# A new order table for the same operations: gated linear recurrence followed by a gMLP block

## The chip, the cores and the metric

The kernel runs on one core of a Trainium2 chip. The metric is the device time of one execution in microseconds (us). The kernel before took 147.5 us, the median of three runs (146.93, 147.5 and 147.93). Its profile comes from a further execution, whose span, from the first instruction to the last, is 146.7 us. Times inside the profile are counted from the start of that span.

## The reference, cut to what matters

```python
def _attn_ref(q, k, v, alpha):           # all (4, 8, 768, 48)
    for t in range(S):
        state = alpha[:, :, t, :, None] * state + np.einsum('bhd,bhe->bhde', k[:, :, t], v[:, :, t])
        y[:, :, t] = np.einsum('bhd,bhde->bhe', q[:, :, t], state)

def _moe_ref(x, w_in, w_spatial, b_spatial, w_out):   # x is y as (4, 768, 384)
    h = np.maximum(x @ w_in, 0.0)        # (4, 768, 1024): u and v, 512 each
    v_n = (v - mu) / np.sqrt(var + 1e-06)
    v_s = np.einsum('ts,bsd->btd', w_spatial, v_n) + b_spatial[None, :, None]
    return ((u * v_s) @ w_out).astype(np.float32)
```

A recurrence over 768 steps with a decay for each of 48 rows of the state, for 4 batches and 8 heads, is followed by a block that mixes over time (w_spatial is 768 x 768) and projects back to 384.

## The kernel before, in words

**Tiling.** The recurrence is cut into 24 chunks of 128 time steps, six for each batch. Chunks 0 to 5 are worked in pairs, with loads of 384 KB for two chunks; chunks 6 to 23 are worked singly, each with four loads of 192 KB: `ac` (alpha), `kc` (k), `qc` (q) and `vc` (v). A single load brings rows of 48 numbers, 192 bytes each. Six weight loads of 768 KB and 24 stores of 192 KB make up the rest of the transfers. All but a 1.5 KB one are issued by SyncE into one queue, in one order.

**Operations.** The body makes no schedule. It builds a list of 1108 operations, each with a key, the engines that may do it, and what it depends on. For chunk i the ones that matter here are:

- `ln.i` (ScalarE, from `ac`), then `cum.i` (TensorE, the decay sums), then three exponentials on ScalarE;
- `kt.i` (GpSimd, from `kc`) and `qt.i` (VectorE, from `qc`), then `trk.i` (TensorE, eight transposes, those of k first), `ev.i` (copy out), `sc.i` (scores, TensorE), `m.i` (mask, VectorE);
- `vb.i` (GpSimd or ScalarE, from `vc`), then `upd.i` (TensorE, from `kt` and `vb`), `z.i` (VectorE), `S.i` and `sb.i` (GpSimd): the state of chunk i as weights for chunk i+1;
- `y.i` (TensorE, from `m.i`, `vb.i` and `sb.(i-1)`), then `xs.i`, `xt.i`, `xe.i`: the output turned into the layout that the second part reads.

For batch b the second part has `v.b.t` (6 products with half of w_in, each with statistics `bn`, `rs`, `vn`), `u.b.f.h` (8 products with the other half), `s.b.f.h` (8 products with w_spatial, each in two parts of three matmuls), `g.b.f.h` (the gate, GpSimd or VectorE) and `o.b.t` (6 products with w_out), followed by the store `st.b.t`. An output tile waits in a buffer until it is stored; the pool `outp` has four of them, and tile (3,0) takes the buffer of tile (2,2).

**Order.** `replay` walks through the string `PLAN`. A word is a letter for the engine and the number of the operation: `G758` emits operation 758, which is `kt.17`, on GpSimd. `S749` is the issue of the load `kc.17`, and the word `Q750` stands where the planner had the transfer itself begin. Numbers after a colon are columns of matmuls on a constant tile, with no use for the result, that are put on TensorE ahead of the operation (`fill`, line 188). Every engine runs its words in the order of the string; what an engine waits for, all behind it waits for. The table was computed ahead of time by a planner that isn't in the file. It used the durations that the operations carry, among them

```python
    LD, LP, WT, ST = 1.03, 1.46, 2.35, 0.8
```

for the transfer of a single-chunk load, of a pair load, of a weight load and of a store. These numbers are data for the planner; the emitted program doesn't use them.

Lines that the profile names: 188 constant-tile matmuls, 361 `xt`, 417 and 616 `ln`, 464 and 646 `kt`, 471 and 656 `qt`, 602 single load, 672 and 674 `trk`, 690 `upd`, 704 `sc`, 732 and 726 `y`, 778 all products of the second part, 332 `S`, 198 copies on VectorE and GpSimd (`vb`, `sb`, `ev`), 933 `g`, 980 store.

Of the kernel before, what the change touches and what calls it, by code (L numbers as in the profile page):

```python
# [54 lines left out]
LETTERS = {"P": "PE", "D": "DVE", "A": "ACT", "G": "POOL", "S": "SP", "Q": "DMA"}  # L55

PLAN = """
S34 S96 G0 S36 S38 Q35 D1 Q97 S100 A42 Q37 S98 P43:512:512:512:512:512:512:512:512:512:352 A104 G32 P54:512 Q33 A44
Q39 S40 P116 A55 D47 A56 P105:128 A57 G58 A45 A46 D2 Q101 S166 P50:512:96 A107 A106 P61:256 A117 D51 A118 A108 D59
A119 Q99 S102 D48 P63:512:512:512:512 A64 D121 P243:512:224 P52 D110 P125 Q41 S4 D53 D62 A126 P73:512:512:160 G120  # L60
P114 A244 D74 P76 Q167 G109 S168 P123:160 D115 D75 A49 G60 P112:512:512:192 D77 Q103 A113 P65:224 S170 D78 A124
P135:512 D66 A174 P79:96 D136 G67 Q5 S172 P138 A80 D137 G68 P69:224 A111 D70 G122 D139 P83:512:352 G71 D140 P175 G72
Q169 S9 P127 A177 A84 P81 D128 P141 A82 G129 A176 P85 Q171 S303 P186 A142 D7 G6 A86 P131 D8 A178 P143 D130 G179 A187
P87 Q173 S14 A188 D132 P90 A88 G133 D180 P145 A91 G189 D190 Q10 S305 A144 P182 D92 P184 A146 G134 P194 A185 P149
D195 G181 A183 D89 P147 P192 G191 A148 P200 G3 Q304 A193 S307 P245:128 D201 P160 A150 D202 Q15 P203 P196 D12 A13 D11
A246 D205 P156:512:512:512:512:320 S18 A93 P154 D197 A311 Q306 S309 D204 A161 G198 P152 A157 P312 D16 Q308 G199 S335
A155 P206 D151 A313 G17 Q19 A153 P210 D94 A314 A207 G315 D162 S22 P158 A316 P208 A211 P233 D317 A209 P231 D95 A163
P212 Q310 P319 D232 S337 A213 P214 D164 A234 G20 D320 Q336 P223 S370 A215 G21 D159 P217 Q23 D216 S339 P227 A218 P235
A224 P237 D219 A228 P225 A318 P229 D165 A343 Q338 D236 S341 P325 A220 D238 P321 A226 P344 Q371 D222 P259 A230 S372
D221 P251 A346 A345 D326 Q340 A24 G25 P255 S374 D322 P256 D327 A348 Q342 P260 G347 S412 D257 P239 A378 Q373 P328  # L70
G323 P241 S410 A240 D349 P379 P252 Q375 D261 A380 S414 P247 A381 D242 A329 G262 Q413 P248 A350 D253 S376 A383 P351
D249 G324 Q411 P353 P330 D352 S26 P267 A331 G258 P268 D384 Q415 S445 P357 G382 D269 P275 Q377 A418 D354 S416 P276
D359 G355 P386 Q27 D358 G356 S447 P271 D387 P419 G254 P272 A421 D277 A420 P392 A423 G422 P332 D424 P360 D273 G250
Q446 A333 S449 P426 D393 A361 P263 G274 A385 Q417 D394 P264 S477 A427 P388 P362 D265 Q448 P395 S479 A363 D31 P432
G266 D30 A396 P364 Q450 D29 A28 S481 D389 A453 D334 P397 P279 G390 Q478 A398 S572 G391 A365 P454 D433 P399 Q480 A455
D434 G278 S451 A456 A458 P408 A400 Q482 P283 D459 G425 S574 A280 D401 G457 P404 A284 Q573 P287 S604 A485 D409 G270
A405 Q452 P428 D366 P486 A288 S576 P435 A487 P461 Q575 A436 G488 S483 P291 A367 D462 A489 Q605 P295 D369 S578 A292
D429 P437 D490 A296 Q577 P467 G430 S606 A438 P406 D368 G431 A580 D469 P492 Q484 A407 S608 P581 D468 G460 P439 A582
Q579 D493 A583 S641 A585 P463 G584 P470 D464 A612 Q607 P494 D586 A471 S639 P402 G465 D495 A440 P472 Q609 G466 P613
A403 D496 S679 P588 A615 A614 G491 P299 D441 Q642 A473 S610 G587 A617 P497 G616 D589 Q640 P474 A498 S681 D618 A442  # L80
P590 P499 Q680 D591 P594 A500 S715 P620 G592 D596 A300 Q611 P501 A475 D443 S645 A476 D621 P514 Q682 P508 S643 D595
A502 P512 A503 Q716 G619 D444 S683 D515 P626 A647 P597 D504 P524 Q646 A513 S717 P528 A598 A509 Q644 D627 P540 S685
A505 P648 A687 P599 D507 Q684 P510 A600 D506 S719 P688 A649 D628 P525 Q718 A650 A690 A652 G651 S747 P541 D526 A723
P622 Q686 P529 D542 A689 G593 S749 A692 P544 D623 D530 Q720 A654 G691 P545 S751 D693 P629 D653 Q748 G624 P724 S841
P695 D511 A725 G543 P655 A630 Q750 D546 P516 S873 A726 A728 G527 P631 D696 A656 Q752 P517 S721 G625 P657 D729 P601
A632 Q842 D658 A694 G531 S843 D518 P661 A602 P701 Q874 D662 P633 G727 A755 S845 D663 P520 Q722 A634 G519 D702 S875
P756 P521 A757 Q844 D703 G659 P664 S877 P536 D522 G758 A665 Q846 P731 D635 A759 S753 P532 G660 A849 Q876 D760 P666
P697 S912 G547 P533 A667 D698 A732 Q878 P537 D534 S908 G523 P704 D538 P850 Q754 A705 P668 D603 G699 S948 A851 P762
A852 Q913 A854 G853 S847 P677 A669 D855 P706 Q909 A730 P548 G700 D678 S301 A707 D763 P733 Q949 P857 A549 D734 S879
A881 P708 D858 G735 A670 Q848 P737 S983 G535 P764 A709 D739 P863 Q302 P671 A710 S914 G736 D738 Q880 P552 S910 A636  # L90
D765 G761 P740 A672 Q984 G539 D766 P882 S950 A741 P556 A553 D864 Q915 G856 P767 S1015 A557 D865 P742 P560 A884 A768
Q911 D711 A883 S952 P673 A886 G885 P564 Q951 A743 D887 S985 A916 P769 D637 G888 P859 A561 Q1016 P675 D674 G923 S954
A770 P744 D676 A712 Q953 P777 D860 S987 A745 D638 P889 G861 Q986 A565 P771 S1019 A956 D890 A778 P779 Q955 D746 A772
S289 P917 P891 P957 A919 Q988 A918 D713 P866 S989 D714 A959 P781 A780 G920 D773 A921 Q1020 P793 S1021 A867 P797 D892
A1023 Q290 D922 P568 A774 S293 Q990 A958 P924 S1017 D776 A961 P785 D775 G960 Q1022 A782 D925 P868 S285 P786 A869
D962 G893 P794 Q294 A963 D787 G862 P798 A569 Q1018 D795 A991 P870 S570 G788 D799 S297 Q286 P926 A871 P895 D927 G796
P930 Q571 D897 P801 Q298 G894 P802 D896 P783 D932 G928 P992 D931 P789 A994 A993 P898 D803 A784 G995 P1024 A996 P966
P933 A899 D967 P790 D997 A934 G968 P809 A1025 D791 G998 A1027 P900 P810 D872 G1026 A901 P964 D1028 P999 G800 A965
P813 D1000 G792 P935 P1030 D811 A936 P814 D1031 G804 P1001 P817 D1002 G929 D815 P970 A818 P1005 D971 P1032 G1003
P942 G1029 D972 P821 G816 D1006 P805 A822 D1007 G969 P973 P937 D1033 A974 G1004 P806 D1034 A938 P975 P1008 D807 A976  # L100
P902 D943 A1009 G808 D939 P1035 A903 P1010 P977 G812 A1036 D904 P944 A978 P940 A1011 D979 P1037 P829 A1038 D945 A905
P825 D907 P1012 A826 A980 P1039 A941 D981 P1049 A1013 D982 P946 D906 A1040 D1014 P1045 A830 P1051 A947 S831 D1041
A1046 P1047 S281 P1053 S823 D1050 A1042 Q832 S558 P1057 A1052 D1044 Q282 S827 P1077 A1048 D1043 Q824 S562 P1065 Q559
P1078 S819 P1066 Q828 P1061 Q563 D1067 P1054 Q820 G1068 P1058 D1055 P1062 D1059 G1056 P1069 D1060 P1070 D1063 P1073
D1079 P833 P1074 A834 P1081 D1075 S835 P1082 D1064 S550 G1076 P837 S554 D1071 Q836 S566 P1084 D1080 A838 Q551 G1072
P1088 S839 Q555 D1083 A1085 P1092 Q567 S1086 A1089 Q840 P1100 S1090 A1093 Q1087 P1096 S1094 A1101 Q1091 P1104 S1102
A1097 Q1095 S1098 A1105 Q1103 S1106 Q1099 Q1107
"""


# [973 lines left out]
```

## Time and profile before

| what | value | where |
|---|---|---|
| time | 147.5 us (146.93 to 147.93) | three runs |
| TensorE busy | 138.6 us of 146.7 | page, first part |
| first and last TensorE matmul | 1.32 us, ends at 143.02 us | chain of waits |
| transfers | 28.61 MB, 93,014 packets, 87,872 of them under 512 B | transfers |
| median single load, issue to landing | 3.8 to 4.2 us | issues |
| median store from `o_sb`, issue to landing | 2.4 us | issues |
| granted TensorE clock | 0.997 | run's record |

In the page, the first part gives busy time by engine and the second the same in 40 slices of 3.67 us, as tenths; `DMA` is the mean busy share of the 16 transfer engines. A matmul's busy time includes its way through the array, so that neighbours overlap: a full slice says that work was under way, and the pace is read from the distance of starts. In the list of stretches, `x` is the number of instructions, `DMA share` the busy share of the transfer engines. In the list of instructions by time, a bracket gives the idle time of the engine before the instruction and what ended it.

### The profile page before, as it was taken

To read this page: it belongs to the slowest core of one execution; us is meant where nothing else is said; L and a number is where in the kernel's file an instruction comes from. 1 tells how busy PE (TensorE), PEld (TensorE's weight loads), DVE (VectorE), ACT (ScalarE), POOL (GpSimd) and SP (SyncE) were. 2 spreads that over 40 slices of the span, in tenths; PEclk is the share of its full clock that TensorE was granted. 3 is DMA by queue.
4 is the path that set the end of the run, shared out by engine and by line. 5 is a ranking of instruction groups with operands and counts; after the bars stand their busy time and mean duration, and the time that the engine had idled before them with its cause. 6 is when DMAs were issued, how large, how long until landed. Compare 5 with 4: busy or idle time off the path is not lost.

```text
span 146.7 us, 4486 instructions
## 1 busy us (share of the span) xinstructions
PE 138.6 (94%) x1702; PEld 92.3 (63%) x1715; DVE 120.6 (82%) x260; ACT 107.8 (73%) x271; POOL 87.1 (59%) x148
## 2 busy tenths in 40 slices
PE   6999999999999999995998999999999999999990
PEld 3567776676666666773666577666667766566550
DVE  6578989979999899994977898988989999767820
ACT  3595779988984599995996889999948548860160
POOL 5726487574258959773139987853597994004320
PEclk9999999999999999999999999999999999999998
DMA  4999998978997999997998999999998000063384
GB/s 109 268 261 263 330 259 245 332 183 210 312 216 151 267 208 199 197 197 141 191 213 163 221 194 206 186 210 188 202 222 258 22 0 0 4 242 138 135 293 161
DMA packets 93014, 28.61 MB, mean 195 GB/s; under 512 B 87872, under 2 KB 91456, under 8 KB 92992
## 3 DMA queue, kind: packets, MB, share of 16 engines
q1 hardware_dynamic: 92960, 28.32, 83.4%
q8 instruction: 13, 0.21, 0.6%
q14 instruction: 9, 0.07, 0.2%
q0 software_dynamic: 32, 0.00, 0.0%
HBM read 23.60 MB, written 4.72 MB: 193 GB/s over the span
## 4 chain that ended last, share of the span: by engine, by line
PE 64%; DMA 12%; DVE 8%; ACT 5%; POOL 4%; issue 3%; SPq 1%; DVEq 0%; ACTq 0%; POOLq 0%
PE bank L778 38%; DMA qc<-in_q_dram 7%; PE bank L188 6%; DMA raw_w<-in_moe_w_spatial_dram 5%; PE bank L704 2%; POOL gT L933 2%; PE bank L672 2%; PE bank L732 2%; PE bank L361 2%; PE bank L674 2%; PE bank L690 1%; DVE qt L656 1%; PE bank L492 1%; PE bank L428 1%; SPq L602 1%
## 5 line engine op out<-in xcount | busy, mean ns | idle before, releaser
L778 PE MATMUL bank<-w_spT,vn 128*128 128x384 bf16 x192 | 36.3, 326 | 0.0
L933 POOL TENSOR_TENSOR gT<-vsb,uT 128x384 bf16<-128x384 f32 x28 | 25.8, 932 | 16.1 <-DVE vsb L920 15.5
L778 PEld LDWEIGHTS <-vn 128*128 128x128 bf16 x192 | 17.3, 97 | 10.0 <-issue 0.2
L715 DVE TENSOR_TENSOR ptm<-bank,mask 128x512 bf16<-128x512 f32 x36 | 22.8, 681 | 0.5 <-PE bank L704 0.5
L646 POOL TENSOR_TENSOR kt<-kc,binv 128x384 bf16<-128x384 f32 x18 | 16.7, 928 | 7.4 <-ACT bc L641 4.4
L920 DVE TENSOR_TENSOR vsb<-bank,bsp_bc 128x384 f32<-128x384 f32 x31 | 16.7, 552 | 3.8 <-PE bank L778 2.8
L778 PE MATMUL bank<-xT,w_in 128*128 128x384 bf16 x96 | 19.2, 327 | 0.0
L778 PE MATMUL bank<-w_out_sb,gT 128*128 128x384 bf16 x96 | 18.4, 326 | 0.1
L778 PE MATMUL bank<-w_in,xT 128*128 128x512 bf16 x59 | 17.1, 379 | 1.0 <-issue 0.5
L332 POOL TENSOR_TENSOR state<-state,bc 128x192 f32<-128x192 f32 x20 | 10.2, 511 | 8.2 <-DVE state L327 4.9
L198 POOL CAST sbd<-state 64x192 bf16<-64x192 f32 x38 | 12.9, 340 | 2.0
L196 ACT COPY xT<-bank 128x384 bf16<-128x384 bf16 x24 | 11.7, 487 | 3.0 <-PE bank L361 2.4
L839 DVE BATCH_NORM_STATS2 stats<-v_sb 128x6 f32<-128x512 bf16 x20 | 13.6, 682 | 0.3 <-ACT v_sb L202 0.3
L202 ACT ACTIVATE v_sb<-bank 128x512 bf16<-128x512 f32 x20 | 11.7, 598 | 2.6 <-PE bank L778 2.2
L656 DVE TENSOR_TENSOR qt<-qc,bank 128x384 bf16<-128x384 f32 x18 | 9.8, 548 | 4.4 <-DMA qc<-in_q_dram 2.9
L188 PE MATMUL bank<-junk 128*128 128x384 bf16 (+5 forms) x66 | 11.8, 313 | 1.3 <-DVE junk L231 1.3
L198 DVE COPY kqT<-bank 128x1024 bf16<-128x1024 bf16 (+1 forms) x19 | 11.6, 614 | 1.5 <-PE bank L674 0.5
L196 ACT COPY o_sb<-bank 128x384 f32<-128x384 f32 x9 | 4.3, 480 | 11.4 <-PE bank L778 11.4
L778 PEld LDWEIGHTS <-w_in 128*128 128x128 bf16 x96 | 8.7, 98 | 6.1
L778 PEld LDWEIGHTS <-gT 128*128 128x128 bf16 x96 | 9.0, 97 | 5.4 <-issue 0.3
L196 ACT CAST x_sb<-bank 128x384 bf16<-128x384 f32 x24 | 11.6, 488 | 1.0 <-PE bank L732 0.5
L871 DVE TENSOR_SCALAR vn<-v_sb,mvs,rstd 128x512 bf16<-128x512 bf16 x24 | 10.6, 467 | 2.0 <-ACT rstd L864 1.9
(124 smaller groups left out, 299.1 us busy)
## 6 DMA issues: line engine op xcount, KB each, us to landing
ac<-in_alpha_dram SPq DMA_DIRECT2D x18, 192.0 KB, 4.1
kc<-in_k_dram SPq DMA_DIRECT2D x18, 192.0 KB, 3.9
qc<-in_q_dram SPq DMA_DIRECT2D x18, 192.0 KB, 3.8
vc<-in_v_dram SPq DMA_DIRECT2D x18, 192.0 KB, 4.2
raw_w<-in_moe_w_spatial_dram SPq DMA_DIRECT2D x3, 768.0 KB, 7.6
out_dram<-raw_w SPq DMA_DIRECT2D x12, 192.0 KB, 2.3
out_dram<-o_sb SPq DMA_DIRECT2D x9, 192.0 KB, 2.4
raw_w<-in_moe_w_in_dram SPq DMA_DIRECT2D x2, 768.0 KB, 7.6
```

The source lines that it names most:

```text
L188: nc.tensor.matmul(out=flat[:, 0:n], lhsT=junk[:, 0:128], rhs=junk[:, 0:n], start=True, stop=True)
L196: nc.scalar.copy(out=out, in_=in_)
L198: ENG[eng].tensor_copy(out=out, in_=in_)
L202: nc.scalar.activation(out=out, in_=in_, func=AF.Relu)
L646: ENG[eng].tensor_mul(out=k_blocks(kt3)[:, :, :, 0:D], in0=quad(st["kc"]), in1=st["binv"])
L656: nc.vector.tensor_mul(out=qt[:, :, ::-1, 0:D], in0=quad(st["qc"]), in1=st["cv"])
L715: nc.vector.tensor_tensor(out=st["ptm"][:, s], in0=st[f"pt{s}"], in1=mask4, op=ALU.mult)
L778: return lambda ps: nc.tensor.matmul(out=out(ps), lhsT=lhsT(), rhs=rhs(), start=start, stop=stop)
L839: nc.vector.bn_stats(out=stats, in_=d["v_sb"][:, tt, :])
L871: nc.vector.tensor_scalar(out=d["vn"][:, t, :], in0=d["v_sb"][:, t, :], scalar1=d["mvs"][:, t, 0:1], scalar2=d["rstd"][:, t:t + 1], op0=AL ...
L920: nc.vector.tensor_tensor(out=hold["vs"], in0=ps[:, 0:TH], in1=bsp_bc[:, th, :], op=ALU.add)
L933: ENG[eng].tensor_tensor(out=bt[b]["gT"][:, dsl, cols], in0=hold["vs"], in1=bt[b]["uT"][:, dsl, cols], op=ALU.mult)
```

## The change

The string `PLAN` is replaced by another one for the same 1108 operations; nothing else in the file changes. The new table comes from a planner run with longer times for single-chunk loads and for stores; the constants in the file are as they were. It is meant to fit the order to transfers that take longer than the old table took for granted. The diff replaces 50 lines by 50 others; its beginning:

```diff
-S34 S96 G0 S36 S38 Q35 D1 Q97 S100 A42 Q37 S98 P43:512:512:512:512:512:512:512:512:512:352 A104 G32 P54:512 Q33 A44
-Q39 S40 P116 A55 D47 A56 P105:128 A57 G58 A45 A46 D2 Q101 S166 P50:512:96 A107 A106 P61:256 A117 D51 A118 A108 D59
...
+S34 S96 G0 S36 S40 Q35 D1 Q97 S38 A42 D2 Q37 S100 P54:512:512:512:512:512:512:512:512:512:352 A104 G32 P43:512 Q33
+Q41 S98 P116:512 A44 A55 P105:128 G47 A118 Q39 S166 A106 G58 A49 P50:512:512:192 A57 A51 Q101 G60 S102 A45 A46
...
```

With numbers turned into names, the order of SyncE where the two tables differ most, from the 45th transfer on:

```
before: qc.12 vc.11 vc.12 kc.13 qc.13 kc.14 ac.14 ac.15 vc.13 kc.15 ac.16 vc.14 qc.14 qc.15 kc.16 vc.15 qc.16 ac.17 kc.17 qc.17 ac.18
after:  qc.12 vc.11 ac.14 qc.13 kc.13 vc.12 qc.14 kc.14 ac.15 ac.16 vc.13 ac.17 kc.15 qc.15 vc.14 ac.18 vc.15 kc.16 qc.16 qc.17 kc.17
```

The words of TensorE and GpSimd around chunk 15 (`s.1.3.1/1` is the second part of that product):

```
TensorE before: s.1.0.1 xt.14 upd.15 s.1.0.1/1 s.1.1.1/1 y.15 cum.18 v.2.2 trk.17 u.2.3.0 xt.15 o.1.0
TensorE after:  xt.14 trk.16 sc.15 u.2.0.0 v.2.2 u.2.1.0 upd.15 trk.17 y.15 cum.18 u.2.3.0 o.1.0 xt.15
GpSimd before:  sb.13 g.1.3.0 kt.16 g.1.0.0 S.14 kt.17 sb.14 g.1.3.1 g.1.1.0 S.15 kt.18 sb.15 S.16 g.1.0.1 sb.16
GpSimd after:   vb.15 kt.16 g.1.2.0 kt.17 S.14 sb.14 g.1.0.0 vb.16 g.1.2.1 kt.18 S.15 vb.17 sb.15 g.1.3.1 S.16 sb.16
```

And the end of TensorE's list:

```
before: s.3.3.1 s.3.3.1/1 o.2.5 o.3.0 o.3.1 o.3.2 o.3.4 o.3.3 o.3.5
after:  s.3.2.1/1 s.3.1.1/1 o.3.0 o.3.1 s.3.3.1/1 o.3.2 o.3.3 o.3.4 o.3.5
```

A few operations change engine where the list allows two: one `sb` on VectorE becomes four, eleven `ev` on ScalarE become fourteen, three gates on VectorE become two, eight weight casts on VectorE become seven. The constant-tile matmuls go from 16,224 to 16,704 columns.

## The prediction

> **What bounds the kernel now.** I read the page first, its busy times and its slices.
>
> ```profile
> PE 138.6 (94%) x1702; PEld 92.3 (63%) x1715; DVE 120.6 (82%) x260; ACT 107.8 (73%) x271; POOL 87.1 (59%) x148
> ...
> PE   6999999999999999995998999999999999999990
> ...
> DMA  4999998978997999997998999999998000063384
> ```
>
> Two things are full: TensorE nearly everywhere, and the transfer engines until about 112 us, when the last load lands. TensorE has one hole, slice 19, near 67 us. The stretches of ten microseconds (columns: TensorE, weight loads, VectorE, ScalarE, GpSimd, clock, transfer share, GB/s) show it as 8.32 of 10, while transfers go on:
>
> ```profile
> 60.00:70.00 10.00, 8.32 (x124) 5.91 (x125) 7.79 (x18) 8.31 (x24) 6.00 (x13) 1.00 0.92 177
> 70.00:80.00 10.00, 9.63 (x108) 6.16 (x106) 8.04 (x20) 8.50 (x26) 4.88 (x9) 1.00 0.96 189
> 80.00:90.00 10.00, 9.89 (x125) 6.83 (x127) 9.08 (x19) 8.64 (x20) 8.99 (x14) 1.00 1.03 201
> ```
>
> The instructions by time name the waits inside:
>
> ```profile
> 68.36 0.36 PE L690 MATMUL bank<-vb,kt 128*128 128x48 bf16 x8 [1.09 <-POOL vb L198]
> ...
> 69.67 0.38 PE L672 MATMUL bank<-ident,kt 128*128 128x128 bf16 x4 [0.46 <-DVE qt L656]
> ...
> 79.47 0.40 PE L674 MATMUL bank<-ident,qt 128*128 128x128 bf16 x4 [0.30 <-DVE qt L656]
> ```
>
> The chain of waits (start, duration) runs through two loads there, and after them through TensorE alone:
>
> ```profile
> 63.81 5.16 DMA qc<-in_q_dram
> ...
> 73.89 4.87 DMA qc<-in_q_dram
> 78.86 1.03 DVE qt L656 x2
> ...
> 125.97 17.06 PE bank L778 x101
> ```
>
> So the end is TensorE's own work plus the time for which loads held it up.
>
> **The ledger.** I add up TensorE's words in table order at the pace of dense stretches, start to start: three 384-column matmuls 0.49 us, four 0.65 (the chain's last run is 101 in 17.06), `v` 0.65, `trk` 0.44, the eight matmuls of `upd` or `y` 0.20 and four more of `y` 0.17, `xt` 0.17, `sc` 0.26 (0.35 paired). `s` 31.4, `u` 15.6, `v` 15.6, `o` 15.6, `y` 10.1, `trk` 8.0, `sc` 6.8, all else 21.8: 124.9 us. Constant-tile matmuls, 16,224 columns at 384 in 0.16 us, make it 131.7. TensorE ends at 143.02, so its **lag**, end minus work listed up to there, is 11.3 us. Followed through the table, the lag is 3.8 after the cold start, 7.0 at 50 us and 7.75 at `v.1.4` (67 us). Then it jumps: 9.0 at `upd.12`, 9.7 at `trk.13`, 10.6 at `trk.14` (80 us). It creeps to 11.0 by 105 us and 11.3 at the end. The jumps, 2.8 us, are what late loads cost.
>
> **What the skill says.** Trainium Architecture — The Big Picture (Inside one NeuronCore): engines run their own instruction streams and meet only at semaphores. The waits above agree: `qt` late by a load stops TensorE for 0.46 us though it has products listed behind. DMA: Bandwidth & Descriptors (Specifications): line rate wants 512 bytes or more a piece. The trace agrees: 37 single loads of 192-byte rows landed from 55.5 (`kc.10`) to 93.1 us (`qc.20`), 1.016 us each; seven stores of equal size but 1536-byte rows landed 0.5 us apart near 131 to 134 us. TensorE: Matmul & The Clock Gate (What you observe) has starts of 128-column matmuls 56 ns apart when warm; the transposes here are 56 ns apart.
>
> **The change, part by part.**
>
> *Constant-tile matmuls.* 480 more columns: +0.2 us, on the path, since TensorE is.
>
> *Engine swaps and operations.* All work stays. Swaps move a handful of 0.3 to 0.9 us copies between engines at 59 to 82%; nothing on the path, taken as 0.
>
> *Loads against TensorE.* In the old table TensorE's words between `Q` of `kc.10` and `Q` of `qc.20` come to 33.5 us for 37 loads, 0.905 each, against 1.016 that they take: TensorE gains on its loads by 37 x 0.111 = 4.1 us, and once its lead is used up it waits. In the new table, 37 loads from `ac.11` to `qc.20` have 35.9 us of TensorE work, 0.970 each: it gains 1.7 us. The bandwidth isn't changed, only the mix.
>
> To find what remains I take each load's landing, the operations queued behind it on its engine, and the consumer on TensorE. The landing is that of the same place in the queue before: the first 46, 65, 72 and 76 transfers are the same sets in both tables, and both are kept busy by SyncE, which issues some 4 us ahead. Lag needed = ready time minus TensorE work listed ahead. On the old table: `qc.15` lands at 78.8, `qt.15` and `qt.14` 0.47 each on VectorE, for `trk.14`'s q half with 69.7 listed ahead: 10.1 to 10.3. The trace has 10.6, so the ledger is 0.25 short. Later peaks are 10.1 (`vc.20` over `vb.20`, `S.18` to `upd.19`) and 10.4 (`kc.23` over `kt.23` and two gates to `o.2.0`): below the lag reached, hence no more jumps.
>
> On the new table the highest is `kc.17`, 65th in the queue. That place landed at 86.0 before, 85.5 when landings around it are evened out. GpSimd has `kt.17` (0.92 start to start), `S.14` (0.5), `sb.14` (0.77) in this order: 87.8, and `y.15` on TensorE needs `sb.14` with 78.7 listed ahead. Lag 9.1. GpSimd's next twelve words keep it at 9.0 to 9.2 as far as `sb.16` and `y.17` (85.8 listed). After that no load asks for more than 8.0. Next below is `ac.15` over `ln.15`, `rs`, `xe.12` to `v.2.0`: 8.3. So late loads now bring the lag to 9.2 + 0.25 = 9.45, not 10.6.
>
> *Stores.* Two stand before `vc.23` in both tables. Afterwards ten go out in a row, the last being `st.2.2`, whose buffer `o.3.0` needs. From `o.2.5` copied out at about 130.6, seven issues at 0.5 and 2.2 to land end at 136; `o.3.0` is ready near 138. Hidden behind batch 3's products.
>
> *The end.* `o.3.3` stands one group (0.65) after the last `s` part instead of 2.6 us; its fourth matmul starts 1.1 us after that part, and the VectorE gate before it takes 0.54 plus some 0.1 to 0.2. Hidden by little. The 3.7 us from TensorE's end to the span's end (two half copies of 0.33 and 0.36, the store) stay.
>
> *Sum.* Lag 9.45 at `y.17`, plus creep of 0.3 and 0.35 at the end as before: 10.1. TensorE ends at 131.9 + 10.1 = 142.0 rather than 143.0. Time 147.5 - 1.0 = **146.5 us**.
>
> **The rivals.**
>
> *A, the chain over `kc.17` doesn't bind.* If it lands at 85.0 or earlier, as single landings scatter by -0.6 to +0.9 about the line, `v.2.0` at 8.3 + 0.25 is the peak; creep from there 0.6, end 0.35: lag 9.5. 131.9 + 9.5 + 3.7 = 145.1 against 146.7: 145.9. If `v.2.0`'s chain is on time too and the lag creeps on from 7.75 alone, it is a further 0.8 less: 145.1. I take 145.7, nearer the first. For: 0.970 is close to 1.016. Against: GpSimd has 6.7 us listed for six of TensorE's at that place.
>
> *B, the waits only move.* Loads are the same stream, and a peak of 10.6 forms elsewhere: 147.5 + 0.2 = 147.7. Against: the ledger names every peak before and finds none now.
>
> *C, slower: another engine becomes the bound.* VectorE has 6.2 us of words for six of TensorE's (48 to 54 listed), where the old table had 4.9; it was 92 to 94% busy at 40 to 60 us already. If B's waits remain and VectorE adds 0.7 while the short end adds 0.9 (a whole `o` group and its copy): 147.7 + 1.6 = 149.3. For: an end with 0.3 us to spare. Against: over 42 to 66 VectorE has 0.97 of TensorE's time, not more.
>
> **How the numbers follow.** Forecast 0.45 (146.5), A 0.28 (145.7), B 0.15 (147.7), C 0.12 (149.3). Predicted time 146.5. The range goes from 144.9, a little under A's lower end, to 148.3, B with half of C's additions. Faster by over 1% means under 146.0: nearly all of A, 0.27, and a third of the forecast, whose own scatter is about 0.7 us, 0.14, make 0.41; slower by over 1%, above 149.0: 0.12, C; same 0.47.
>
> **What would show it.** In the changed profile: the 60 to 70 stretch near full on TensorE; no wait of 1 us on `vb`; a wait of about 1 us at `y.15` (line 726) near 87 us, ended by GpSimd's `sb`; last loads at 112 us as before; TensorE ending near 142. It is wrong if the lag at `y.17` is not 9 to 10, if VectorE or ScalarE ends waits of over 0.5 us between 50 and 66 us, or if the last `o` groups have gaps.

## The result: 1.1% slower, and the profile after

The changed kernel took 149.18 us (median of four runs, 149.07 to 149.41) against 147.72 us (146.93 to 148.13) for the kernel before on the same chip: a ratio of 1.0108, 95% interval 1.0061 to 1.0154 (the two medians alone give 1.0099). Executions of one kernel can fall into a fast and a slow group; the times here are medians of the fast ones. The profiled execution has a span of 147.5 us, where the kernel before had 146.7. TensorE ends at 143.76 us, not at 142.0 as forecast, and not at 143.02 as before.

The page of the changed kernel, busy times and slices:

```profile
PE 138.9 (94%) x1702; PEld 91.7 (62%) x1716; DVE 120.0 (81%) x261; ACT 109.7 (74%) x274; POOL 85.7 (58%) x144
...
PE   6997989999989999998999999999999999999990
...
DVE  6708789899996999999999887999877958776721
...
DMA  4999999989998997998999998995980026019344
```

The hole in TensorE's row near 67 us, a 5 before, is an 8 now; a 7 and two 8s are new near 13, 20 and 42 us. Stretches of ten microseconds, columns as before (TensorE, weight loads, VectorE, ScalarE, GpSimd, clock, transfer share, GB/s):

```profile
50.00:60.00 10.00, 9.80 (x141) 6.81 (x143) 9.72 (x21) 8.95 (x23) 8.78 (x14) 1.00 0.93 211
60.00:70.00 10.00, 9.14 (x112) 5.90 (x111) 9.50 (x20) 9.76 (x29) 5.05 (x8) 1.00 1.00 195
70.00:80.00 10.00, 9.89 (x118) 6.65 (x119) 9.32 (x22) 7.15 (x23) 4.16 (x8) 1.00 1.00 199
```

TensorE is busier from 60 to 70 us, 9.14 where it had 8.32, and GpSimd has a microsecond less to do. VectorE went from 7.79 to 9.50 and ScalarE from 8.31 to 9.76. Between 45 and 71 us the waits for loads have all but gone (`vb` waited 1.9 us for `vc` and `qt` 2.0 us for `qc`; 0.3 us for `vc` is left). TensorE's longest waits there (who waited for whom: total, times, longest) name VectorE's copy:

```profile
PEld L704 <- DVE kqT L198: 1.8, 3, 0.6
...
PE bank L704 <- DVE kqT L198: 0.7, 2, 0.5
```

The chain of waits (start, duration) has lost both loads of 63.81 and 73.89 us. One load stands in it earlier, `qc` from 33.94 us. From 54 to 65 us it runs through VectorE, with only short visits elsewhere:

```profile
33.94 5.43 DMA qc<-in_q_dram
...
54.21 0.68 DVE kqT L198
54.89 0.52 DVE qt L656
55.41 1.26 DVE ptm L715 x2
...
61.31 0.61 DVE stats L839
...
63.01 0.95 DVE sbd L198
...
125.52 18.25 PE bank L778 x109
```

So the load waits of 60 to 80 us went, as forecast, and others took their place. The ledger of the prediction, worked on each trace in the same way (largest lag so far, us, at that much listed TensorE work), says where. The last two rows belong to experiments e2 and e3:

| listed work | 9 | 24 | 48 | 60 | 72 | 84 | 96 | end |
|---|---|---|---|---|---|---|---|---|
| before | 4.48 | 5.92 | 7.36 | 9.00 | 10.58 | 10.84 | 10.85 | 11.33 |
| after | 5.22 | 6.57 | 8.09 | 9.85 | 10.34 | 10.65 | 11.33 | 11.87 |
| before, whole-row loads | 4.33 | 6.08 | 7.37 | 7.75 | 8.39 | 8.91 | 8.92 | 9.40 |
| after, whole-row loads | 5.22 | 6.54 | 7.91 | 9.53 | 10.01 | 10.32 | 11.00 | 11.54 |

The kernel before pays 2.8 us in three jumps from 58 to 72 (listed), the changed one pays in small pieces from the start: 0.7 more by 9, and 2.1 between 45 and 60 (`sc.9` 0.24, `xt.10` 0.31, `sc.11` 0.33, `sc.12` 0.62 and crumbs). At 72 they are level. The 0.5 us by which the new lag ends higher come between 84 and 96, again in crumbs of 0.1 to 0.2 at `y.17`, `trk.19`, `o.1.4` and `s.2.1.0`. After 96 the two lose alike (0.48 and 0.54 us), some 0.2 us of it at `s.3.3.1` in both. The other 0.2 us of TensorE's later end is the added columns.

### The profile page after: what moved, and what is told of

The parts are those of the page before. It is cut to its first block, busy times and chain, and to the rows that moved or that the text cites. A ratio compares the mean times of both kernels' runs of the same rounds, so it can differ in the third digit from the quotient of the medians.

```text
span 147.5 us, 4476 instructions
## 1 busy us (share of the span) xinstructions
PE 138.9 (94%) x1702; PEld 91.7 (62%) x1716; DVE 120.0 (81%) x261; ACT 109.7 (74%) x274; POOL 85.7 (58%) x144
## 4 chain that ended last, share of the span: by engine, by line
PE 76%; DVE 10%; DMA 4%; ACT 3%; POOL 3%; issue 2%; SPq 0%; DVEq 0%; POOLq 0%
PE bank L778 44%; PE bank L188 6%; DMA qc<-in_q_dram 4%; PE bank L704 3%; PE bank L672 2%; PE bank L361 2%; PE bank L674 2%; PE bank L732 2%; DVE ptm L715 2%; PE bank L690 2%; PE bank L492 2%; PE bank L622 2%; PE bank L726 2%; PE bank L428 1%; PE bank L546 1%
## 5 line engine op out<-in xcount | busy, mean ns | idle before, releaser
L933 POOL TENSOR_TENSOR gT<-vsb,uT 128x384 bf16<-128x384 f32 x29 | 26.7, 927 | 18.2 <-DVE vsb L920 16.5
L715 DVE TENSOR_TENSOR ptm<-bank,mask 128x512 bf16<-128x512 f32 x36 | 23.6, 682 | 3.3 <-PE bank L704 3.1
L332 POOL TENSOR_TENSOR state<-state,bc 128x192 f32<-128x192 f32 x20 | 10.5, 524 | 16.2 <-DVE state L325 9.0
L778 PE MATMUL bank<-xT,w_in 128*128 128x384 bf16 x96 | 19.7, 326 | 0.0
L188 PE MATMUL bank<-junk 128*128 128x384 bf16 (+7 forms) x67 | 11.4, 313 | 2.3 <-DVE junk L231 1.3
L196 ACT COPY kqT<-bank 128x512 bf16<-128x512 bf16 (+1 forms) x14 | 10.5, 769 | 3.4 <-PE bank L492 1.6
L198 POOL CAST sbd<-state 64x192 bf16<-64x192 f32 x32 | 11.3, 352 | 1.7
L202 ACT ACTIVATE uT<-bank 128x384 bf16<-128x384 f32 x22 | 10.4, 490 | 1.3 <-PE bank L778 1.2
L198 DVE COPY kqT<-bank 128x1024 bf16<-128x1024 bf16 (+1 forms) x16 | 9.8, 617 | 1.8 <-PE bank L492 0.9
```

The costliest lines, as they stand in the source:

```text
L188: nc.tensor.matmul(out=flat[:, 0:n], lhsT=junk[:, 0:128], rhs=junk[:, 0:n], start=True, stop=True)
L196: nc.scalar.copy(out=out, in_=in_)
L198: ENG[eng].tensor_copy(out=out, in_=in_)
L202: nc.scalar.activation(out=out, in_=in_, func=AF.Relu)
L332: ENG[eng].tensor_tensor(out=st["state"], in0=st["state"], in1=st["bc"][:, :, None].to_broadcast([128, HP, D]), op=ALU.mult)
L715: nc.vector.tensor_tensor(out=st["ptm"][:, s], in0=st[f"pt{s}"], in1=mask4, op=ALU.mult)
```

## The experiments

Each ratio is to the kernel before on the same chip; the experiments ran on four chips. "Stretch" is the time from the end of `sc.8` to the end of `sc.12`, which in the changed order holds 16.57 us of listed TensorE work.

| run | us | ratio (95%) | stretch, us |
|---|---|---|---|
| changed kernel | 149.18 | 1.0108 (1.0061 to 1.0154) | 18.69 |
| e1, two casts on GpSimd | 149.69 | 1.0157 (1.0123 to 1.0192) | 18.93 |
| e2, before, whole-row loads | 146.06 | 0.9928 (0.9897 to 0.9958) | |
| e3, after, whole-row loads | 148.74 | 1.0095 (1.0062 to 1.0129) | 18.54 |
| e4, before up to 30 us | 149.64 | 1.0150 (1.0104 to 1.0195) | 18.53 |
| e5, before with new loads | 151.72 | 1.0280 (1.0240 to 1.0321) | |
| e6, after with old loads | 159.91 | 1.0845 (1.0803 to 1.0888) | 21.01 |
| e7, before up to 12 us | 154.34 | 1.0472 (1.0437 to 1.0506) | 18.54 |
| e8, before up to 22 us | 148.46 | 1.0081 (1.0058 to 1.0105) | 18.90 |
| e9, old engines | 153.57 | 1.0426 (1.0395 to 1.0457) | 20.19 |
| e10, the same, whole rows | 153.91 | 1.0447 (1.0417 to 1.0477) | 20.13 |
| e11, `sc.12` later | 149.96 | 1.0185 (1.0156 to 1.0214) | (moved) |
| e12, four moves | 150.65 | 1.0231 (1.0198 to 1.0263) | (moved) |
| e13, rows, casts cut | 148.66 | 1.0070 (1.0045 to 1.0096) | 18.42 |
| e14, rows, ScalarE cut | 148.72 | 1.0074 (1.0046 to 1.0102) | 18.54 |
| e15, rows, both cut | 148.59 | 1.0073 (1.0048 to 1.0099) | 18.38 |
| e16, rows, `o.0.5` ahead | 148.94 | 1.0086 (1.0060 to 1.0112) | (moved) |
| e17, rows, three waits cut | 148.72 | 1.0015 (0.9991 to 1.0039) | 17.91 |
| e18, rows, chain cut | 148.58 | 0.9987 (0.9958 to 1.0016) | 17.88 |

The chip of e17 and e18 ran the kernel before at 148.63 us, the others at 147.2 to 147.7. So these two ratios can't be set beside the rest, and the traces have to speak.

### What the loads cost each order

```diff
-nc.sync.dma_start(out=t, in_=src[b, :, t0:t0 + C, :].rearrange("h s d -> s h d"))
+nc.sync.dma_start(out=t.rearrange("s h d -> s (h d)"),
+                  in_=src[b].rearrange("h (s r) d -> (h s) (r d)", r=8)[t0:t0 + C, :])
```

> The kernel before, with the single-chunk loads reading the same number of bytes as whole rows of 1,536 bytes (the values land permuted, so the attention works on other numbers; no other work changes). Theory A (late single-chunk loads cost the kernel before 2.8 us at upd.12, trk.13 and trk.14): those three jumps go, the lag at trk.15 falls from 10.3 to about 8, and the time from 147.7 to 145-146.5. Theory B (behind the loads stand waits of other engines that take their place): the jumps go, but the lag at the end is within 0.5 us of 11.3 and the time within 0.5 us of 147.7.

> The changed kernel with the same edit of the single-chunk loads. Theory A (its loads no longer bind, VectorE and the early part do): time within 0.4 us of 149.2, lag at the end 11.6-12.0. Theory B (loads still hold it somewhere, directly or by slowing the other engines): 0.7 us or more shorter.

In both, the loads of the middle chunks land more than ten microseconds earlier: `kc.14` lands at 54.7 us in e2 (69.9 in the kernel before) and at 57.8 in e3 (70.9 in the changed kernel). The stretch of e2 that held the hole:

```profile
60.00:70.00 10.00, 9.87 (x136) 6.84 (x137) 9.58 (x21) 9.54 (x28) 6.83 (x14) 1.00 0.90 278
```

TensorE is at 9.87 there. The same stretch of e3 has hardly changed from the 9.14 above:

```profile
60.00:70.00 10.00, 9.29 (x113) 5.99 (x111) 9.50 (x20) 9.91 (x29) 5.00 (x7) 1.00 0.78 226
```

Late loads cost the kernel before 1.4 us (147.43 to 146.06, same chip) and 1.9 us of lag; they cost the changed kernel 0.3 us of lag. Without late single-chunk loads the new order is 2.7 us slower than the old one (148.74 against 146.06, same chip). In the traces TensorE ends 2.3 us later, of which 2.1 are lag and 0.2 the added columns. That is the size of what was overlooked.

> The compute order of the kernel before with the load and store order of the changed kernel (only the order in SyncE's queue differs from before). Theory A (the earlier loads are the whole good of the change, and the rest of it the harm): the jumps at upd.12, trk.13 and trk.14 (2.35 us together) shrink to under 1 us, the lag at the end falls from 11.3 to 9.4-10.4, the time from 147.5 to 145.8-146.8. Theory B (when a load lands is set by its buffer's release or by the DMA rings, not by its place in the queue): jumps and time as before, within 0.4 us of 147.5.

> The compute order of the changed kernel with the load and store order of the kernel before. Theory A (the changed kernel's loads had slack): late loads appear, 0.5-2 us more than 149.2. Theory B (VectorE's pace up to 70 us hides them): within 0.4 us of 149.2.

Both are far slower than either theory had it. In e5 `o.0.0` loses 1.93 us to w_out, which now comes four transfers later, and the first `qt` 1 us for `qc.0`, which comes one later; in e6 the first chunk's `upd.0` loses 3.55 us, since its `vc.0` comes later. In these tables the order of loads and the order of operations are made for each other; "the loads alone" isn't a part that can be taken out. In e5 the loads landed no faster as a whole: of the loads of chunks 12 to 17, those that the new order prefers land up to 8 us earlier than in the kernel before (`ac.17`, 74.6 for 82.5), others up to 1.6 us later (`kc.16`, 81.0 for 79.4).

### Is the lag inherited from the start?

VectorE's first multiplication starts at 7.68 us in the kernel before, and at 11.08 in the changed one. The two aren't alike: the first is a `kt`, which the new table gives to GpSimd; the first `qt` of the kernel before starts at 9.82 us. The changed kernel, VectorE by time:

```profile
11.08 0.56 DVE L471 TENSOR_TENSOR qt<-qc,bank 128x384 bf16<-128x384 f32 x1 [4.52 <-ACT bank L453]
```

The loss of about a microsecond at `tr.k.0.1` comes from there, as far as the trace tells: at 12.54 us constant-tile matmuls ahead of it end a wait of 0.95 us for the second `qt`, which starts at 11.93 because ScalarE's exponential for it starts at 11.39 (7.99 before). No run changed this alone. Three kernels take the first words of the old table and then the new table's order for the operations that are left (83, 171 and 237 words).

> The order before for its first 83 words (up to y.0, 11.6 us of listed TensorE work), the changed order for the rest; the loads keep the changed order from there on. Theory C (VectorE paces TensorE from 15 to 70 us, and in the changed kernel it is 2 us behind because it got its first work at 11.08 us instead of 7.68): VectorE's idle time by 15 us falls from 11.2 to about 9, the lag at sc.12 from 9.75 to 8-8.8, the time to 147.5-148.5. Theory D (what VectorE and GpSimd are given between 25 and 60 us sets the lag, whatever came before): lag at sc.12 9.5 or more, time within 0.4 us of 149.2.

> The same with the order before up to sc.2.1 (21.7 us listed). Theory C: as for the splice at 12 us, lag at sc.12 8-8.8 and 147.5-148.5 us. Theory D: lag at sc.12 9.5 or more and the time within 0.4 us of 149.2.

> The order before up to v.0.5 (29.9 us of listed TensorE work), then the changed order for what is left. If the jumps at tr.k.0.1 (+1.03) and xt.0 (+0.34) of the changed kernel carry its loss, the lag at v.0.5 is 6.2 instead of 6.6, stays lower to the end, and the time is 148.0-148.7. If VectorE between 45 and 70 us sets the lag whatever stands before, the lag at sc.12 is again 9.7 and the time within 0.2 us of 149.2.

Theory C fell, though none of the three is clean: at the seam loads come in neither table's order. In e4, VectorE by time shows it:

```profile
41.90 0.55 DVE L656 TENSOR_TENSOR qt<-qc,bank 128x384 bf16<-128x384 f32 x1 [1.93 <-DMA qc<-in_q_dram]
```

What they do show is in the stretch. It is entered at 50.2 us in e3, at 50.9 in e4 and at 55.1 in e7, and it takes 18.54, 18.53 and 18.54 us. (In e8 it takes 18.90, with a load, `vc` from 52.21 to 59.60 us, in its chain of waits.) A kernel that arrives five microseconds late loses the same two microseconds over again. The loss is made in the stretch, by the new table's own order and engine choices.

### Engine choices

> The changed kernel with two of its state casts (sb.7 and sb.10, 1.14 and 1.22 us on VectorE) put back on GpSimd; nothing else moves. Theory A (VectorE sets TensorE's pace between 45 and 70 us because it was given more work, the two casts above all): VectorE loses 2.4 us of work there, TensorE's lag at sc.12 falls from 9.75 to 8.7-9.2 us, and the time from 149.2 to 148.3-148.8 us. Theory B (the early losses at tr.k.0.1 and xt.0 and the rest of the order carry it): lag at the end and time within 0.2 us of the changed kernel.

```diff
-D356 ... D466
+G356 ... G466
```

VectorE has 25.96 us of work from `sc.8` to `sc.14` instead of 27.84, and nothing is gained. The waits of e1 between 45 and 71 us tell why:

```profile
PEld L703 <- DVE kqT L197: 1.5, 2, 0.9
...
DVE vsb L919 <- POOL gT L932: 1.2, 2, 0.8
```

GpSimd, already 98% busy from `sc.8` to `sc.9` (99% in e1), falls behind with the gates; VectorE waits for it to free a `vsb` buffer, and its next `kqT` comes 0.5 us later than before, counted from `sc.8`.

> The changed order, word for word, but every operation on the engine that it had in the kernel before (52 operations go back, 9 of them between sc.8 and sc.12). Theory F (the engine choices of the new table carry the 2 us that TensorE loses between sc.8 and sc.12): the stretch sc.8 to sc.12 (18.69 us for 16.57 listed in the changed kernel) falls to 17.6, time 148.2-148.7. Theory G (the new order itself carries it, through round trips TensorE to VectorE or ScalarE and back with too little other TensorE work between): 18.5 or more, time within 0.4 us of 149.2 or longer, since the order was planned for its own choices.

> The same with the single-chunk loads as whole rows, so that no load can bind (against 148.7 us for the changed kernel with such loads). Theory F: stretch sc.8 to sc.12 down from 18.54 to about 17.5, time 147.5-148.0. Theory G: stretch 18.3 or more and 148.4 us or more.

Between the two tables 55 operations change engine, not 52; the counts given with the change are what is left when swaps both ways cancel. Both kernels are much slower, so theory F has no support. But this isn't a measure of the choices alone: TensorE is held up near 20 us, and its granted clock drops. The stretch itself, run at full clock, is 20.2 us with VectorE at 0.81 and ScalarE at 0.85: with engines less full, TensorE waits more. In its chain of waits from `sc.8` to `sc.14` ScalarE has 10.5 us and VectorE 3.0. Each operation now comes up at another place in another engine's queue, which is a likely reason, not a tested one. The choices belong to the order that was planned with them.

> The changed kernel with whole-row loads (148.7 us, stretch sc.8 to sc.12 18.54 us), and the state casts sb.7 and sb.10 cut from 48 columns a head to 4 (what they leave out, the products of those two chunks miss): VectorE loses about 2 us of work and GpSimd gains none. Theory I (VectorE and ScalarE are each full in a part of the stretch, one after the other): only VectorE's parts shorten, stretch 17.9-18.2, sc.11 to sc.12 stays at 3.3-3.4 with ScalarE at 1.00, time 148.1-148.5. Theory J (VectorE alone): stretch 17.4 or less and 147.6 or less. Theory K (neither; TensorE's own order): 18.4 or more.

> The changed kernel with whole-row loads, and seven ScalarE operations ahead of sc.12 (the exponentials of chunks 10 to 13 and the logarithms of 11 to 14) cut to a quarter of their columns: ScalarE loses about 1.8 us there, VectorE none. Theory I: sc.11 to sc.12 falls from 3.37 to 3.0 or less, stretch 17.9-18.2, time 148.1-148.5. Theory J: stretch 18.4 or more. Theory K: 18.4 or more.

> Both cuts together. Theory I: more than either alone and about their sum, stretch 17.0-17.5, time 147.2-147.9. Theory J: as with VectorE alone. Theory K: 18.4 or more.

e13 was meant to relieve VectorE and hardly did. These are its casts, with 16 columns instead of 192, and GpSimd beside them:

```profile
49.98 0.99 DVE L198 CAST sbd<-state 64x16 bf16<-64x16 f32 x2
```

```profile
50.03 1.79 POOL L933 TENSOR_TENSOR gT<-vsb,uT 128x384 bf16<-128x384 f32 x2
```

A pair that should take a third of a microsecond takes 0.99; the changed kernel's full pair there takes 1.14. Their time is GpSimd's, as told at the end. ScalarE did lose its work in e14 (from 17.42 to 16.25 us in the stretch), and the stretch stayed at 18.54. So ScalarE alone doesn't set it. In e15 the stretch is 0.16 us shorter, too little to show in the time; what it says comes with e17 and e18 below.

### TensorE's own order

At `sc.12` every variant of the new order so far loses 0.62 us, whatever its lag. TensorE in the changed kernel, by time:

```profile
67.44 0.39 PE L674 MATMUL bank<-ident,qt 128*128 128x128 bf16 x4
67.66 0.33 PE L726 MATMUL bank<-sbd,kqT 128*128 128x96 bf16 x4
67.83 0.36 PE L732 MATMUL bank<-vb,ptm 128*128 128x48 bf16 x8
68.68 0.40 PE L704 MATMUL bank<-kqT 48*128 48x128 bf16 x8 [0.48 <-DVE kqT L198]
```

Between `trk.12` (first line) and `sc.12` (last) stands only `y.11`, 0.37 us of listed work; the old table has 2.03 us. VectorE's copy in between takes 0.7 us, and the handovers come on top. That looked like the cause (theory K), and three kernels put more work there.

```diff
 y.11
+o.0.5        (e16; in e11 sc.12 goes behind xt.11 and o.0.5 instead)
 sc.12
 xt.11
-o.0.5
```

> The changed kernel with sc.12 moved behind xt.11 and o.0.5 in TensorE's queue, so that 0.8 us of ready work lies in the round trip trk.12, ev.12, sc.12. Theory G: the jump of 0.62 at sc.12, which stands in every variant whatever its lag, goes; the lag at 63 us listed falls from 9.85 to 9.2-9.4, the time to 148.5-148.9. Theory H (VectorE and ScalarE are full there at 0.96 and 0.94 of the stretch, so the wait is only moved): the lag is back at 9.7-9.9 by 66 us listed and the time within 0.3 us of 149.2.

> The changed kernel with four such moves: upd.6 behind wt.3, sc.9 behind xt.8, xt.10 behind o.0.1, sc.12 behind o.0.5. Theory G: four jumps (0.52, 0.24, 0.31, 0.62) go or shrink, the end lag falls by 1 us or more, the time to 147.8-148.4. Theory H: each wait comes back at one of the next operations, lag at 66 us listed 9.8 or more, time within 0.3 us of 149.2.

> The changed kernel with whole-row loads, o.0.5 moved from behind xt.11 to between y.11 and sc.12 in TensorE's queue (xt.11 stays behind sc.12). If TensorE's own order is what costs the 0.62 us at sc.12 (theory K): no jump there, time 148.1-148.4. If the helper engines are full (theory I): the lag at 66 us listed is again 9.7-9.9 and the time within 0.3 us of 148.7.

In e16 the jump at `sc.12` is gone, and 0.35 and 0.31 us appear at `u.1.1.1` and `y.12`, 0.66 together; from `sc.8` to `sc.14` it needs 29.19 us, e3 29.09. In e11 `xt.11` loses 0.96 us to ScalarE. e11, e12 and e17 also lost some 0.65 us at `tr.q.0.0` near 16 us, ahead of any word that differs, so I use their jumps and stretches rather than their ends. The last two take the waits away, by other data, with all work kept:

```diff
-lhsT=st["kqT"][rows, hp, :], rhs=st["kqT"][rows, HP + hp, :]
+kq = T[i - 1 if i in (9, 11, 12) else i]["kqT"]      # e18: i in (8, ..., 13), and ptm in y likewise
+lhsT=kq[rows, hp, :], rhs=kq[rows, HP + hp, :]
```

> The changed kernel with whole-row loads, in which sc.9, sc.11 and sc.12 read the kqT of the chunk ahead of theirs (other numbers, same work), so that TensorE needn't wait there for the copy that VectorE has just begun. Theory K (the round trip itself, with 0.37 us of TensorE work between trk.12 and sc.12 where the order before has 2.03): the jumps at sc.9, sc.11 and sc.12 (0.24, 0.33, 0.62) go, the stretch sc.8 to sc.12 falls from 18.54 to 17.3-17.7, the lag at 66 us listed from 9.83 to 8.7-9.1, the time from 148.7 to 147.6-148.0. Theory H (engines in their own order, with VectorE at 0.96, take back what one wait gives): the waits come back at y, xt or u within a few us, lag at 66 us listed 9.5 or more, time within 0.3 us of 148.7.

> The same for all of chunks 8 to 13, and y of these chunks reads the ptm of the chunk ahead: TensorE's chain through VectorE (transposes, copy, scores, mask, product) is cut, the work of every engine stays. Theory K: stretch sc.8 to sc.12 17.2 or less, lag at 66 us listed 8.6 or less, 147.5 us or less. Theory H: VectorE and ScalarE hold TensorE through the banks that they release and the other operands, stretch 18.2 or more, time within 0.4 us of 148.7.

TensorE in e18, by time:

```profile
67.31 0.40 PE L704 MATMUL bank<-kqT 48*128 48x128 bf16 x8
68.28 0.34 PE L361 MATMUL bank<-ident,x_sb 128*128 128x128 bf16 x3 [0.58 <-ACT x_sb L196]
```

`sc.12` doesn't wait, and the next operation, `xt.11`, waits for ScalarE's copy as long as `sc.12` did for VectorE's. The stretch to `sc.12` fell by 0.65 us, and at that next operation it is all back. These are the whole 29 us from `sc.8` to `sc.14`, 26.64 us of listed TensorE work, in e3, e17 and e18 (one line from each; columns as above):

```profile
50.21:79.30 29.09, 28.07 (x355) 18.84 (x360) 27.68 (x59) 25.09 (x70) 17.10 (x28) 1.00 0.66 210
```

```profile
50.79:79.87 29.08, 28.04 (x355) 18.86 (x360) 27.61 (x59) 25.10 (x70) 17.17 (x28) 1.00 0.70 218
```

```profile
49.83:78.90 29.07, 27.99 (x354) 18.82 (x360) 27.59 (x59) 25.11 (x70) 17.16 (x28) 1.00 0.66 216
```

29.09, 29.08, 29.07: theory H. All three have 27.6 us of work on VectorE, 1.04 times TensorE's 26.64, and 25.1 on ScalarE. But VectorE alone doesn't hold them. In the chain of waits over these 29 us VectorE has 7.28 us and ScalarE 0.90 in e3; in e18 VectorE has 0.95 and ScalarE 7.67. At the end of the stretch two copies stand side by side: VectorE's `ev.12`, for `sc.12`, and ScalarE's `xs.11`, for `xt.11` (us after the end of `sc.8`):

| run | `ev.12` ends | `sc.12` starts | `xs.11` ends | `xt.11` starts |
|---|---|---|---|---|
| e3 | 18.08 | 18.14 | 18.40 | 18.47 |
| e13, casts cut | 17.97 | 18.03 | 18.39 | 18.44 |
| e14, ScalarE cut | 18.08 | 18.14 | 18.17 | 18.47 |
| e15, both cut | 17.92 | 17.98 | 18.01 | 18.31 |
| e17, three waits cut | 17.98 | 17.51 | 18.40 | 18.45 |
| e18, chain cut | 17.97 | 17.48 | 18.40 | 18.45 |

ScalarE's `xs.11` by time in e3 (first) and in e15:

```profile
68.09 0.52 ACT L195 CAST x_sb<-bank 128x384 bf16<-128x384 f32 x1
```

```profile
67.32 0.48 ACT L196 CAST x_sb<-bank 128x384 bf16<-128x384 f32 x1
```

When `sc.12` comes earlier (e13, e17, e18), `xt.11` waits for `xs.11`; when `xs.11` comes earlier (e14), `xt.11` still stands behind `sc.12`. Only in e15, where both come earlier, does `xt.11`, by 0.16 us; in e3, e4 and e7 it starts at 18.47 each time. So here the distance from one wait to the next is 0.02 us, and two helpers hold TensorE at once: theory I, on the small scale that e15 tried.

The old order without load waits:

```profile
49.67:80.95 31.28, 30.58 (x392) 20.80 (x397) 28.00 (x61) 28.60 (x78) 21.39 (x35) 1.00 0.65 199
```

There 29.41 us of listed TensorE work stand against 28.00 on VectorE, 0.95, and the stretch costs 1.9 us more than listed rather than 2.4, with a tenth more work in it.

**What is shown and what isn't.** Shown: the single-chunk loads stopped binding from 60 to 80 us; the new table is 2.7 us slower by itself; its largest piece arises between `sc.8` and `sc.12`, isn't inherited from earlier, and doesn't yield to taking away any one wait, to ScalarE's relief or to VectorE's at GpSimd's cost. At the end of that stretch VectorE and ScalarE hold TensorE within 0.02 us of each other, and only relieving both brought it forward. That the same pair carries all of the 2 us is an inference: e15 took only 0.16 us off VectorE's side, and no run put the lighter ScalarE of e14 together with the cut chain of e18. Nor is VectorE's share of work a measure of the pace: at 0.81 (e9) the stretch took longer. The loss at the start is read from the trace alone, and for the 0.7 us after 84 listed no cause was tried. No order tried here beat the kernel before; e2 did, but it reads other numbers, and only measures what the loads cost.

## Why the prediction was wrong, step by step

- **What bounds the kernel now.** Right as far as it went: TensorE, plus late loads. The 2.8 us of jumps were the size of the waits, not what removing them brings: without any (e2) the lag falls by 1.9 us and the time by 1.4. Other waits stood close behind.
- **Constant-tile matmuls, +0.2 us.** Right: listed work went from 131.7 to 131.9.
- **"Engine swaps and operations. All work stays ... nothing on the path, taken as 0."** This is the step that failed. All work does stay, but its place moves, and only the loads were followed through the table. For every other engine the step rested on busy shares. The runs put the term at 2.5 us of time (e3 against e2, less 0.2 for the columns) and at 2.1 us of lag: 0.9 at the start, 1.2 from 48 to 60 us listed and 0.7 after 84, with 0.8 regained in between. The swaps aren't a handful: 55 operations change engine. In the table's own terms, 0.37 us of TensorE work between `trk.12` and `sc.12` instead of 2.03 could be read beforehand, though e16 and e17 show that this place alone doesn't carry the loss. The two new casts were counted among copies of 0.3 to 0.9 us; they took 1.14 and 1.22.
- **Loads against TensorE, peak at `y.15` through `kc.17`, lag 9.45.** The direction was right, the place wrong. `kc.17` landed at 84.0 us, 1.5 to 2 us ahead of the place in the queue that it was given, and no wait appeared at `y.15`. The loads' remaining cost is 0.3 us of lag (e3), all of it before 60 us listed; by then TensorE is behind by 9.85, mostly for other reasons.
- **Stores; the end.** Hidden, as said; the 3.7 us after TensorE's end stayed 3.7. The short end cost nothing: the 0.2 us lost at `s.3.3.1` is lost in the kernel before as well.
- **The sum.** TensorE's end 143.76 instead of 142.0: lag 11.87 instead of 10.1. The loads' share of the lag fell from 1.93 to 0.33 us, by 1.6, where the sum has 1.2 (11.3 to 10.1); the term put at nothing added 2.1.
- **Rivals.** C came nearest (149.3). It named VectorE, one of the two engines that took over, but the way was another: it added VectorE and the end to load waits that stayed, while the load waits went and other waits replaced them whole. The evidence against it was 0.97 of TensorE's time from 42 to 66 listed; the trace has 1.04 over `sc.8` to `sc.14`, of which two casts held up beside GpSimd make 1.3 us.
- **What would show it.** The lag at `y.17` is 10.83, outside 9 to 10, as said. The other sign, waits over 0.5 us ended by VectorE or ScalarE between 50 and 66 us, shows in TensorE's weight loads, where the kernel before has none over 0.3:

```profile
54.94 0.23 PEld L704 LDWEIGHTS <-kqT 48*128 48x128 bf16 x8 [0.59 <-DVE kqT L198]
...
62.12 0.17 PEld L361 LDWEIGHTS <-x_sb 128*128 128x128 bf16 x3 [0.52 <-ACT x_sb L196]
...
65.31 0.23 PEld L704 LDWEIGHTS <-kqT 48*128 48x128 bf16 x8 [0.57 <-DVE kqT L198]
```

In the ledger the same places are jumps of only 0.24, 0.31 and 0.33 us, and the one of 0.62 comes at 68.7. Many small waits add up below such a threshold.

## What to carry to other kernels

When an order changes, follow every engine's queue through it, not only the resource that the change is about: for each consumer on the full engine, count how much other work stands between producer and consumer, and compare each helper's work with that engine's over the same words. A wait found on the path is worth no more than the distance to the next wait; running both orders with the suspected resource made cheap shows what stands behind it, here some 2.5 us that the forecast had put at nothing. Where two helpers hold the full engine side by side, relieving one shows nothing; relieve each, then both. Loads, engine choices and operation order of a planned table can't be exchanged one at a time: of seven such mixtures five were 2.8 to 8.5% slower than the kernel before, and none was faster.

## What the runs showed of the hardware

**A VectorE cast begun while a GpSimd gate runs lasts until that gate ends.** In the changed kernel, casts of 64x192 take 253 to 255 ns; the second of `sb.7` took 876 ns and the first of `sb.10` 954, both begun while a gate ran on GpSimd, and both ended 115 and 114 ns after it. In e13 the 64x16 cast took 167 ns alone, and 814 and 870 beside a gate, ending 30 and 28 ns after it. One line for all casts of e13 (shortest, median, longest in ns):

```profile
L198 DVE CAST sbd<-state x8: 167/254/870, 13.0 to 112.4; 64x192 bf16<-64x192 f32 x4, 64x16 bf16<-64x16 f32 x4
```

The Trainium skill, SBUF — State Buffer (Who interferes with whom), offers a reason: VectorE and GpSimd share a pair of ports under "an exclusive lock", which casts and copies of VectorE can take. The runs agree with it, and add that cutting the cast from 192 columns to 16 saved only some 70 ns of it.

**TensorE's clock.** In four experiments the granted clock fell early on. e6, columns as above:

```profile
10.00:15.00 5.00, 1.57 (x24) 0.83 (x21) 0.00 (x0) 1.55 (x6) 0.51 (x1) 0.93 1.29 261
15.00:20.00 5.00, 3.64 (x34) 2.51 (x34) 3.63 (x8) 2.66 (x9) 1.37 (x2) 0.50 1.16 315
```

The five microseconds after the gap run at half clock; e7 falls to 0.57, e9 to 0.61 and e10 to 0.66. The Trainium skill, TensorE: Matmul & The Clock Gate (Part 1: The HAM clock gate), says that the clock halves after an idle window of about 3.4 us. That fits e6, where TensorE waits 3.43 us until 13.98 us. It doesn't account for e9 and e10, whose longest waits in those microseconds are 1.05 and 0.92 us. So part of what e6, e7, e9 and e10 lost is clock, not waits.
